# A retention pair's matmuls put in another order: three changes of tile mode instead of five

## Chip, core and metric

The kernel runs on one core of one Trainium2 chip. The metric is the device time of one execution in microseconds (us). Below, PE is TensorE, DVE is VectorE, ACT is ScalarE, POOL is GpSimd and SP is SyncE, whose queue issues nearly all DMAs of the stage in question.

## Reference

Retention (attention with a decay instead of a softmax) over 4 batches of 8 heads of 64 features and 576 positions; then a gated layer and a layer of eight experts, which the change leaves alone.

```python
scores = scale * np.matmul(q, k.transpose(0, 1, 3, 2))
gamma = 1.0 - 2.0 ** (-5.0 - np.arange(H))
rel = pos[:, None] - pos[None, :]
Dmat = np.where(rel >= 0, gamma[:, None, None] ** rel[None, :, :], 0.0)
ret = np.matmul(scores * Dmat[None], v)
...
x = ret.transpose(0, 2, 1, 3).reshape(B * S, H * D)
x = _moe_ref(x=x, ...)          # RMS norm, silu(x wg) * (x wv), wo
return _moe2_ref(x=x, ...)      # 8 experts, Sinkhorn-normalised weights
```

## The kernel before

The program has three stages: retention (about the first 85 of 2000 us), the gated layer, the experts. Only retention is touched. It goes over 16 pairs of heads (4 batches times 4 pairs); the two heads of a pair lie in partitions 0 to 63 and 64 to 127. The 576 positions are four chunks of 128 and a tail of 64. For pair i the work is:

- `scores(i)`: eight matmuls of a chunk's keys with its queries (contraction 64, output 128 rows, so PE works as tiles of 64 x 128) into `sc`, two PSUM banks; two matmuls for the tail's scores (64 x 64 tiles) into slot 4 of `u`; DVE multiplies `sc` by the masks into `am` (L293).
- `states(i)`: eight matmuls of keys with values (contraction 128, output 64 rows: tiles of 128 x 64) into slots 0 to 3 of `u`; DVE scans them over the chunks into `block_states` (L313) and masks the tail's scores into `mt` (L314).
- `outputs(i)`: the tail's output (from the state and from `mt`, 64 x 64 tiles) into slot 5 of `u`; the states' share of the chunks (64 x 64 tiles) and the masked scores' share (128 x 64 tiles) into `o`, one bank; DVE scales both into `acc` (L342 for the tail, L344 for the chunks).

So one tile `u`, a single PSUM bank of 512 fp32 columns, holds a pair's chunk states, its tail scores and its tail output. `u`, `sc` and `o` have two buffers each, `kT` and `ks` two, `qT` and `vs` three.

The loop of L453 runs one pair ahead: in turn i it records `scores(i + 1)`, `states(i + 1)` and `outputs(i)`, then one step of the gated layer's weight preparation on DVE and ACT (L126 to L146), then a step of the RMS norm where its sums are ready. The order in which this is written is the order on each engine; semaphores follow from which tile is read and written. Two instructions of different engines on one PSUM bank are kept apart by the recording layer, whichever columns they touch. The loads of a turn stand on SP's queue in this order: `qT` and `vs` of pair i + 2, a weight tile where a slot is free, `kT` and `ks` of pair i + 3. Each waits for the last reader of the buffer that it fills, and those behind it wait with it.

Of the kernel before, what the change touches and what calls it, by code (L numbers as in the profile page):

```python
# [13 lines left out]
ALU = mybir.AluOpType  # L14
# [3 lines left out]
B, H, S, D = 4, 8, 576, 64  # L18
# [7 lines left out]
C = 128  # L26
NC = S // C
# [23 lines left out]
def retention_glu_experts(ctx: ExitStack, tc: tile.TileContext, a, out):  # L51
# [6 lines left out]
    nc = tc.nc  # L58
# [43 lines left out]
    def load_weights(most=2):  # L102
        for _ in range(most):
            if n_load[0] == len(sources) or not raw_slots:
                return
            i = n_load[0]
            n = raw_of[i] = raw_slots.pop(0)
            t = rawp.tile([128, 1024], I32, tag=f"raw{n}", name=f"raw{i}")
            nc.sync.dma_start(t, sources[i].bitcast(I32))
            raw[i], asked[i] = t, n_step[0]  # L110
            n_load[0] += 1
# [139 lines left out]
    steps = acc_d[:, :, (B - 1) * S:(B - 1) * S + D * NC]  # L251
# [3 lines left out]
    heads = [slice(h * D, (h + 1) * D) for h in range(2)]  # L255
    loaded, staged, squares = {}, {}, {}

    def load_pair(i, *names, queue=nc.sync):
        if i >= B * NP:
            return  # L260
        b, pr = divmod(i, NP)
        t = {}
        for n in names:
            t[n] = ld.tile([128, a[n].shape[-1]], F32, tag=n, name=f"{n}{i}", bufs=2 if n[0] == "k" else 3)
            queue.dma_start(t[n], a[n][b, pr])
        loaded.setdefault(i, {}).update(t)

    def scale_keys(i):
        if i >= B * NP:
            return  # L270
        for h in range(2):
            hh = 2 * (i % NP) + h
            ks = loaded[i]["ks"].rearrange("p (c h d) -> p c h d", h=2, d=D)[:, :, h, :]
            nc.scalar.mul(ks, ks, g_key[:, hh:hh + 1])

    def scores(i):
        if i >= B * NP:
            return
        pr = i % NP
        t = loaded[i]  # L280
        kt, qt = t["kT"], t["qT"]
        u = psa.tile([128, 512 // D, D], F32, tag="u", name=f"u{i}")
        sc = psa.tile([128, 2, NC, C], F32, tag="sc", name=f"sc{i}")
        am = am_p.tile([128, 2, NC, C], F32, tag="am", name=f"am{i}")
        for c in range(NC):
            for h in range(2):
                hs = slice(h * D, (h + 1) * D)
                cs = slice(c * C, (c + 1) * C)
                nc.tensor.matmul(sc[:, h, c, :], lhsT=kt[hs, cs], rhs=qt[hs, cs], start=True, stop=True)
        for h in range(2):  # L290
            hs = slice(h * D, (h + 1) * D)
            nc.tensor.matmul(u[hs, NC, :], lhsT=kt[hs, NC * C:], rhs=qt[hs, NC * C:], start=True, stop=True)
        nc.vector.tensor_mul(am, sc, masks[:, pr].to_broadcast([128, 2, NC, C]))  # L293
        staged[i] = am, u

    def by_chunk(u):
        return u[:, :NC, :].rearrange("p c d -> p (c d)")

    def states(i):
        if i >= B * NP:  # L300
            return
        pr = i % NP
        t = loaded[i]
        am, u = staged[i]
        ks, vs = t["ks"], t["vs"]
        by_feature = by_chunk(u).rearrange("p (d c) -> p d c", c=NC)
        for c in range(NC):
            for h in range(2):
                cs = slice((2 * c + h) * D, (2 * c + h + 1) * D)
                nc.tensor.matmul(by_feature[h * D:(h + 1) * D, :, c], lhsT=ks[:, cs], rhs=vs[:, cs], start=True, stop=True)  # L310
        st = block_states[i % 2]
        mt = am_p.tile([128, TAIL], F32, tag="mt", name=f"mt{i}")
        nc.vector.tensor_tensor_scan(st, steps[:, pr], by_chunk(u), 0.0, ALU.mult, ALU.add)  # L313
        nc.vector.scalar_tensor_tensor(mt, u[:, NC, :], g_tail[:, pr:pr + 1], causal_t, ALU.mult, ALU.mult)  # L314
        staged[i] = am, mt, st, u

    def outputs(i):
        b, pr = divmod(i, NP)
        t = loaded.pop(i)
        qt, vs = t["qT"], t["vs"]  # L320
        am, mt, st, u = staged.pop(i)
        st = st.rearrange("p (d c) -> p d c", c=NC)
        o = psa.tile([128, NC, C], F32, tag="o", name=f"o{i}")
        ot = u[:, NC + 1, :]
        for hs in heads:
            nc.tensor.matmul(ot[hs, :], lhsT=st[hs, :, NC - 1], rhs=qt[hs, NC * C:], start=True, stop=False)
        for hs in heads:
            nc.tensor.matmul(ot[hs, :], lhsT=vs[hs, 2 * NC * D:], rhs=mt[hs, :], start=False, stop=True)
        for c in range(1, NC):
            for hs in heads:  # L330
                nc.tensor.matmul(
                    o[hs, c, :], lhsT=st[hs, :, c - 1], rhs=qt[hs, c * C:c * C + C],
                    start=c == 1, stop=False, skip_group_check=True,
                )
        for c in range(NC):
            for h, hs in enumerate(heads):
                nc.tensor.matmul(
                    o[hs, c, :], lhsT=vs[:, (2 * c + h) * D:(2 * c + h + 1) * D], rhs=am[:, h, c, :],
                    start=False, stop=c == NC - 1, skip_group_check=True,
                )  # L340
        xf = acc_d[:, pr, b * S:(b + 1) * S]
        nc.vector.tensor_mul(xf[:, NC * C:], ot, g_out[:, pr, :TAIL])  # L342
        yield
        nc.vector.tensor_mul(  # L344
            xf[:, :NC * C].rearrange("p (c i) -> p c i", c=NC), o,
            g_out[:, pr:pr + 1, :].to_broadcast([128, NC, C]),
        )
        sq = sp.tile([128, S], F32, tag="sq", name=f"sq{i}")
        nc.scalar.activation(sq, xf, AF.Square)
        if pr:  # L350
            nc.gpsimd.tensor_add(sq, sq, squares[b])
        squares[b] = sq
        yield
# [93 lines left out]
    scale_keys(0)  # L447
    scale_keys(1)
    scores(0)
    states(0)  # L450
    load_pair(2, "kT", "ks")
    for i in range(B * NP):
        b, pr = divmod(i, NP)  # L453
        load_pair(i + 2, "qT", "vs")
        load_weights(1)
        if i == 2:
            nc.sync.dma_start(rms_g, a["rms_g"])
            nc.sync.dma_start(ident, a["ident"])
            nc.sync.dma_start(wg_raw.rearrange("p k e -> p (k e)"), a["wg"])
        scores(i + 1)  # L460
        states(i + 1)
        load_pair(i + 3, "kT", "ks")
        scale_keys(i + 2)
        out_steps = outputs(i)
        next(out_steps)
        step_weights(load=False, apart=1)
        next(out_steps)
        if i in SUMS_AT:
            next(sums[i // NP - 1], None)
        if i >= 2 * NP - 1:  # L470
            next(norms[0], None)
        if i in (B * NP - 3, B * NP - 1):
            next(norms[1])
# [729 lines left out]
    n, l = len(jobs) - 1, len(jobs) - 2  # L1203
# [108 lines left out]
```

## Time and profile before

| what | us |
|---|---|
| median of 3 runs (lowest, highest) | 2000.55 (2000.46, 2002.4) |
| span of the profiled execution (first to last instruction) | 1999.9 |
| the profiled execution's own time, where a run's time is the span and what lies around it | not listed; 2000.55 less 1999.9 leaves 0.65 |
| PE busy | 1983.4 (99%) |
| DVE busy | 1441.8 (72%) |
| ACT busy | 869.7 (43%) |
| retention's last matmul gives way to the norm's | 84.35 after the start |

PE's busy time includes stretches in which it is slowed by its neighbours, since matmuls are pipelined and their ends are modelled. Times in the rows are counted from the start of the span.

### The profile page before, as it was taken

To read this page: it belongs to the slowest core of one execution; us is meant where nothing else is said; L and a number is where in the kernel's file an instruction comes from. 1 tells how busy PE (TensorE), PEld (TensorE's weight loads), DVE (VectorE), ACT (ScalarE), POOL (GpSimd) and SP (SyncE) were. 2 spreads that over 40 slices of the span, in tenths; PEclk is the share of its full clock that TensorE was granted. 3 is DMA by queue.
4 is the path that set the end of the run, shared out by engine and by line. 5 is a ranking of instruction groups with operands and counts; after the bars stand their busy time and mean duration, and the time that the engine had idled before them with its cause. 6 is when DMAs were issued, how large, how long until landed. Compare 5 with 4: busy or idle time off the path is not lost.

```text
span 1999.9 us, 29898 instructions
## 1 busy us (share of the span) xinstructions
PE 1983.4 (99%) x11390; PEld 1856.2 (93%) x11390; DVE 1441.8 (72%) x2276; ACT 869.7 (43%) x1655; POOL 740.4 (37%) x692
## 2 busy tenths in 40 slices
PE   9999999999999999999999999999999999999998
PEld 7788988988889998999999999999999999999998
DVE  6865555554688777777786777777787777777777
ACT  4453323322454444444444444444445444444443
POOL 3300000000153544545544444545466454444543
PEclk9999999999999999999999999999999999999999
DMA  9411111110178888888888676767767767676773
GB/s 314 150 32 53 50 45 52 44 43 1 48 294 301 291 301 305 308 295 311 303 309 313 245 279 239 276 254 263 265 237 282 264 256 280 237 266 251 271 260 142
DMA packets 111535, 436.56 MB, mean 218 GB/s; under 512 B 11720, under 2 KB 29128, under 8 KB 95008
## 3 DMA queue, kind: packets, MB, share of 16 engines
q1 hardware_dynamic: 109904, 432.39, 59.5%
q8 instruction: 89, 1.46, 0.3%
q10 hardware_dynamic: 1248, 1.49, 0.2%
q0 software_dynamic: 240, 0.79, 0.1%
q14 instruction: 54, 0.44, 0.1%
HBM read 312.41 MB, written 122.21 MB: 217 GB/s over the span
## 4 chain that ended last, share of the span: by engine, by line
PE 95%; DVE 3%; DMA 1%; ACT 1%; POOL 0%; issue 0%; ACTq 0%; SPq 0%; DVEq 0%; POOLq 0%
PE py L751 10%; PE pz L751 10%; PE px L751 10%; PE qx L997 7%; PE qy L997 6%; PE qz L997 6%; PE gv L177 5%; PE gv L179 5%; PE gv L178 5%; PE y L178 4%; PE y L179 4%; PE y L177 4%; PE qz L751 3%; PE x L177 2%; PE x L178 2%; PE x L179 2%
## 5 line engine op out<-in xcount | busy, mean ns | idle before, releaser
L751 PE MATMUL py<-sx,w1s 128*128 128x384 f32 x1152 | 232.0, 335 | 1.1 <-ACT py L1089 0.9
L539 POOL TENSOR_TENSOR t<-rw 128x256 f32<-128x256 f32 x32 | 43.0, 1343 | 508.2 <-DVE sx L576 398.8
L1178 POOL TENSOR_TENSOR acc<-z,a_block 128x384 f32<-128x384 f32 x63 | 64.0, 1015 | 434.7 <-DVE z L1172 434.7
L751 PEld LDWEIGHTS py<-sx,w1s 128*128 128x128 f32 x1152 | 203.0, 188 | 5.3 <-ACT py L1089 2.4
L751 PE MATMUL px<-xhi,w1s 128*128 128x384 f32 x640 | 188.8, 335 | 0.3 <-DVE t L205 0.3
L987 ACT CAST xhi<-acc 128x384 fp32r<-128x384 f32 x316 | 156.0, 514 | 69.8 <-POOL acc L1178 35.4
L991 DVE TENSOR_TENSOR xlo<-acc,xhi 128x384 fp32r<-128x384 f32 x191 | 178.3, 960 | 1.8 <-ACT xhi L987 1.8
L991 POOL TENSOR_TENSOR xlo<-acc,xhi 128x384 fp32r<-128x384 f32 x125 | 145.7, 1165 | 29.7 <-ACT xhi L987 29.7
L1005 DVE TENSOR_TENSOR acc<-acc,qz 128x384 f32<-128x384 f32 x246 | 134.9, 548 | 25.5 <-PE qz L997 25.4
L205 DVE TENSOR_TENSOR t<-t,gv 128x512 f32<-128x512 f32 (+1 forms) x60 | 38.0, 633 | 124.6 <-PE gv L179 123.3
L751 PEld LDWEIGHTS px<-xhi,w1s 128*128 128x128 f32 x640 | 117.9, 188 | 0.9 <-DVE t L205 0.6
L1005 DVE TENSOR_TENSOR acc<-acc,qx 128x384 f32<-128x384 f32 x123 | 67.4, 548 | 71.1 <-PE qx L997 71.1
L751 PE MATMUL pz<-sx,w1s 128*128 128x384 f32 x576 | 115.4, 334 | 0.0
L751 PE MATMUL pz<-xhi,w1s 128*128 128x384 f32 x384 | 113.9, 337 | 0.1
L796 DVE SCALAR_TENSOR_TENSOR acc<-y,prob,acc 128x512 f32<-128x512 f32 x144 | 101.4, 742 | 8.1 <-PE y L179 8.1
L751 PE MATMUL px<-xlo,w1s 128*128 128x384 f32 x320 | 107.0, 334 | 0.0
L1023 ACT COPY qz<-qy 128x384 f32<-128x384 f32 x127 | 58.8, 463 | 106.3 <-PE qy L997 100.5
L179 PE MATMUL y<-xlo,xhi 128*128 128x512 f32 x264 | 103.8, 393 | 0.0
L178 PE MATMUL y<-xlo,xhi 128*128 128x512 f32 x264 | 103.6, 393 | 0.0
L177 PE MATMUL y<-xlo,xhi 128*128 128x512 f32 x264 | 102.6, 389 | 0.0
L751 PEld LDWEIGHTS pz<-sx,w1s 128*128 128x128 f32 x576 | 101.3, 188 | 0.7
L1015 ACT COPY qy<-qx 128x384 f32<-128x384 f32 x127 | 58.8, 463 | 95.2 <-PE qx L997 89.4
(401 smaller groups left out, 5890.9 us busy)
## 6 DMA issues: line engine op xcount, KB each, us to landing
w1s<-w_kept SPq DMA_DIRECT2D x64, 1792.0 KB, 7.2
w_kept<-w1s SPq DMA_DIRECT2D x32, 1792.0 KB, 6.6
rw<-in_w_dram SPq DMA_DIRECT2D x64, 512.0 KB, 5.5
w_kept<-xlo SPq DMA_DIRECT2D x64, 512.0 KB, 3.8
w2s<-w_kept SPq DMA_DIRECT2D x32, 1024.0 KB, 6.8
w_extra<-w_kept SPq DMA_DIRECT2D x32, 768.0 KB, 7.7
w_kept<-xlo SPq DMA_DIRECT2D x44, 384.0 KB, 4.3
w2c<-w_kept SPq DMA_DIRECT2D x32, 512.0 KB, 7.9
```

What stands on the lines that cost most here:

```text
L177: nc.tensor.matmul(ps, lhsT=lh, rhs=rh, start=start, stop=False)
L178: nc.tensor.matmul(ps, lhsT=lh, rhs=rl, start=False, stop=False)
L179: nc.tensor.matmul(ps, lhsT=ll, rhs=rh, start=False, stop=stop)
L751: nc.tensor.matmul(ps, lhsT=l, rhs=r[:, k, :], start=start and k == 0 and i == 0, stop=k == 1 and i == 2, skip_group_check=True,)
L796: nc.vector.scalar_tensor_tensor(o, y_2, pe, o, ALU.mult, ALU.add)
L987: nc.scalar.copy(hi, x)
L991: (engine or nc.vector).tensor_sub(lo, x, f32(hi))
L997: nc.tensor.matmul(ps, lhsT=l, rhs=r, start=start and i == 0, stop=i == 2, skip_group_check=True)
L1005: nc.vector.tensor_add(dst, dst, ps)
L1015: nc.scalar.copy(y, x)
L1023: nc.scalar.copy(z, y)
L1178: nc.gpsimd.tensor_add(sums[0], z[:, 0, :], h_blocks[0])
```

## The change

In a turn the matmuls of both pairs are put in another order. The tail's scores move from `scores` to a second step of `states`, behind the chunk states and their scan. The masked scores' share of the output moves to the front of `outputs`, and is recorded between the two steps of `states`. `states` and `outputs` become generators that the loop steps in turn; the loads of `kT` and `ks` and the scaling of `ks` are recorded between these steps. The accumulation in `o` now starts with the masked share and ends with the states' share. No instruction is added or removed.

```diff
@@ scores
-        for h in range(2):
-            hs = slice(h * D, (h + 1) * D)
-            nc.tensor.matmul(u[hs, NC, :], lhsT=kt[hs, NC * C:], rhs=qt[hs, NC * C:], start=True, stop=True)
         nc.vector.tensor_mul(am, sc, masks[:, pr].to_broadcast([128, 2, NC, C]))
@@ states
         st = block_states[i % 2]
+        nc.vector.tensor_tensor_scan(st, steps[:, pr], by_chunk(u), 0.0, ALU.mult, ALU.add)
+        yield
+        for hs in heads:
+            nc.tensor.matmul(u[hs, NC, :], lhsT=kt[hs, NC * C:], rhs=qt[hs, NC * C:], start=True, stop=True)
         mt = am_p.tile([128, TAIL], F32, tag="mt", name=f"mt{i}")
-        nc.vector.tensor_tensor_scan(st, steps[:, pr], by_chunk(u), 0.0, ALU.mult, ALU.add)
         nc.vector.scalar_tensor_tensor(mt, u[:, NC, :], g_tail[:, pr:pr + 1], causal_t, ALU.mult, ALU.mult)
         staged[i] = am, mt, st, u
+        yield
@@ outputs
+        for c in range(NC):
+            for h, hs in enumerate(heads):
+                nc.tensor.matmul(
+                    o[hs, c, :], lhsT=vs[:, (2 * c + h) * D:(2 * c + h + 1) * D], rhs=am[:, h, c, :],
+                    start=c == 0, stop=False, skip_group_check=True,
+                )
+        yield
         for hs in heads:
             nc.tensor.matmul(ot[hs, :], lhsT=st[hs, :, NC - 1], rhs=qt[hs, NC * C:], start=True, stop=False)
...
                 nc.tensor.matmul(
                     o[hs, c, :], lhsT=st[hs, :, c - 1], rhs=qt[hs, c * C:c * C + C],
-                    start=c == 1, stop=False, skip_group_check=True,
-                )
-        for c in range(NC):
-            for h, hs in enumerate(heads):
-                nc.tensor.matmul(
-                    o[hs, c, :], lhsT=vs[:, (2 * c + h) * D:(2 * c + h + 1) * D], rhs=am[:, h, c, :],
                     start=False, stop=c == NC - 1, skip_group_check=True,
                 )
@@ the loop
         scores(i + 1)
-        states(i + 1)
+        state_steps, out_steps = states(i + 1), outputs(i)
+        next(state_steps, None)
+        next(out_steps)
         load_pair(i + 3, "kT", "ks")
         scale_keys(i + 2)
-        out_steps = outputs(i)
+        next(state_steps, None)
         next(out_steps)
```

Three places show what stands on the engines. The first is PE in turn 2, where pair 3 is scored and pair 2 put out, before the change. A number behind a name is the pair; the words in brackets are the engines or DMA queues whose signal an instruction waits for.

```order
L289 MATMUL sc3_326<-qT3_255,kT3_226 128x128 [waits DMAHW7_49,DMAHW1_49]
L289 MATMUL sc3_326<-qT3_255,kT3_226 128x128 x7
L292 MATMUL u3_325<-qT3_255,kT3_226 64x64 [waits DVE_49]
L292 MATMUL u3_325<-qT3_255,kT3_226 64x64
L310 MATMUL u3_325<-vs3_257,ks3_228 64x64 [waits DMAHW2_49,DMAHW0_49,Activation_49]
L310 MATMUL u3_325<-vs3_257,ks3_228 64x64 [waits Activation_49]
L310 MATMUL u3_325<-vs3_257,ks3_228 64x64 x6
L326 MATMUL u2_261<-qT2_195,block_states0_115 64x64 x2
L328 MATMUL u2_261<-mt2_283,vs2_197 64x64 x2
L331 MATMUL o2_356<-qT2_195,block_states0_115 64x128 x6
L337 MATMUL o2_356<-am2_263,vs2_197 64x128 x8
```

The same turn of PE with the change:

```order
L289 MATMUL sc3_326<-qT3_255,kT3_231 128x128 [waits DMAHW7_49,DMAHW1_49]
L289 MATMUL sc3_326<-qT3_255,kT3_231 128x128 x7
L307 MATMUL u3_325<-vs3_257,ks3_233 64x64 [waits DMAHW0_49,DMAHW2_49,DVE_49,Activation_49]
L307 MATMUL u3_325<-vs3_257,ks3_233 64x64 [waits Activation_49]
L307 MATMUL u3_325<-vs3_257,ks3_233 64x64 x6
L328 MATMUL o2_346<-am2_263,vs2_197 64x128 x8
L312 MATMUL u3_325<-qT3_255,kT3_231 64x64 [waits DVE_49]
L312 MATMUL u3_325<-qT3_255,kT3_231 64x64
L334 MATMUL u2_261<-qT2_195,block_states0_115 64x64 x2
L336 MATMUL u2_261<-mt2_299,vs2_197 64x64 x2
L339 MATMUL o2_346<-qT2_195,block_states0_115 64x128 x6
```

The tail's scores (L292, now L312) moved behind the masked share (L337, now L328), and the first of them waits for a signal of DVE that it did not wait for there. In the built program that signal is the scan's of the same pair: for pair 0 it is DVE's third, after a memset and the mask product, for pair 1 its sixth. The wait that stood on L292, for the buffer of `u`, stands on the chunk states now.

The second place is the end of the stage on PE, pairs 14 and 15, from the scores of pair 15's tail on. Before:

```order
L292 MATMUL u15_1150<-qT15_1071,kT15_1034 64x64 [waits DVE_49]
L292 MATMUL u15_1150<-qT15_1071,kT15_1034 64x64
L310 MATMUL u15_1150<-vs15_1073,ks15_1036 64x64 [waits DMAHW2_49,DMAHW0_49,Activation_49]
...
L326 MATMUL u14_1075<-qT14_1005,block_states0_115 64x64 x2
L328 MATMUL u14_1075<-mt14_1097,vs14_1007 64x64 x2
L331 MATMUL o14_1175<-qT14_1005,block_states0_115 64x128 x6
L337 MATMUL o14_1175<-am14_1077,vs14_1007 64x128 x8
L326 MATMUL u15_1150<-qT15_1071,block_states1_116 64x64 [waits DVE_49]
```

With the change:

```order
L328 MATMUL o14_1171<-am14_1077,vs14_1007 64x128 x8
L312 MATMUL u15_1150<-qT15_1071,kT15_1039 64x64 [waits DVE_49]
L312 MATMUL u15_1150<-qT15_1071,kT15_1039 64x64
L334 MATMUL u14_1075<-qT14_1005,block_states0_115 64x64 x2
L336 MATMUL u14_1075<-mt14_1109,vs14_1007 64x64 x2
L339 MATMUL o14_1171<-qT14_1005,block_states0_115 64x128 x6
L328 MATMUL o15_1207<-am15_1152,vs15_1073 64x128 [waits PE_49]
```

Pair 14's share from the states stood ahead of anything that waits for pair 15's scan, and stands behind it now.

The third place is SP's queue at the loads of pairs 2 and 3. Before:

```order
L265 DMA kT_191<-in_kT_dram 128x576 [waits DMAHW2_49,PE_49]
L265 DMA ks_193<-in_ks_dram 128x512 [waits DMAHW3_49,PE_49,Activation_49]
L265 DMA qT_195<-in_qT_dram 128x576 [waits DMAHW4_49]
L265 DMA vs_197<-in_vs_dram 128x576 [waits DMAHW5_49]
L109 DMA raw_199<-in_gate_dram 128x1024 [waits DMAHW6_49]
L265 DMA kT_226<-in_kT_dram 128x576 [waits DMAHW7_49,PE_49]
```

With the change:

```order
L265 DMA kT_191<-in_kT_dram 128x576 [waits DMAHW2_49,PE_49]
L265 DMA ks_193<-in_ks_dram 128x512 [waits DMAHW3_49,Activation_49]
L265 DMA qT_195<-in_qT_dram 128x576 [waits DMAHW4_49]
L265 DMA vs_197<-in_vs_dram 128x576 [waits DMAHW5_49]
L109 DMA raw_199<-in_gate_dram 128x1024 [waits DMAHW6_49]
L265 DMA kT_231<-in_kT_dram 128x576 [waits DMAHW7_49,PE_49]
```

The order of the queue is the same. The load of `kT` waits, then as now, for the tail's scores of the pair whose buffer it takes; these come later on PE, so a wait of its own of `ks` on PE is no longer needed.

## Rows read from the trace of the kernel before

**Rows 1.** The page, busy time by engine (us, share, instructions).

```profile
PE 1983.4 (99%) x11390; PEld 1856.2 (93%) x11390; DVE 1441.8 (72%) x2276; ACT 869.7 (43%) x1655; POOL 740.4 (37%) x692
```

**Rows 2.** Busy time in two stretches (length; each engine's us and instructions; PEclk, DMA share, GB/s).

```profile
27.04:31.30 4.26, 4.26 (x75) 3.71 (x73) 3.81 (x7) 2.40 (x5) 1.42 (x1) 1.00 0.89 277
...
57.82:81.16 23.34, 21.47 (x354) 18.61 (x354) 23.09 (x43) 12.18 (x25) 7.83 (x6) 1.00 0.59 195
```

**Rows 3.** Timeline, pair 4 scored, pair 3 put out (start, us, instruction, idle before).

```profile
22.79 1.16 PE L289 MATMUL sc<-qT,kT 64*128 64x128 f32 x16
...
23.88 0.33 PE L292 MATMUL u<-qT,kT 64*64 64x64 f32 x4
24.00 1.23 DVE L293 TENSOR_TENSOR am<-sc,masks 128x1024 f32<-128x1024 f32 x1
...
24.14 0.69 PE L310 MATMUL u<-vs,ks 128*64 128x64 f32 x16
...
24.76 0.45 PE L326 MATMUL u<-qT,block_states 64*64 64x64 f32 x4
...
25.05 0.28 PE L328 MATMUL u<-mt,vs 64*64 64x64 f32 x4
...
25.14 0.68 DVE L313 TENSOR_TENSOR_SCAN block_states<-acc,u 128x256 f32<-128x256 f32 x1
25.16 0.93 PE L331 MATMUL o<-qT,block_states 64*64 64x128 f32 x12
25.73 0.26 DVE L314 SCALAR_TENSOR_TENSOR mt<-u,tables 128x64 f32<-128x64 f32 x1
...
26.02 1.09 PE L337 MATMUL o<-am,vs 128*64 128x128 f32 x16
26.04 0.42 DVE L126 TENSOR_SCALAR cv<-cv 128x512 f32<-128x512 f32 x1
...
27.04 0.97 PEld L289 LDWEIGHTS sc<-qT,kT 64*128 64x128 f32 x16 [0.17 <-issue]
...
27.44 0.68 DVE L344 TENSOR_TENSOR acc<-o,g_out 128x512 f32<-128x512 f32 x1
```

**Rows 4.** Timeline, a load of queries on SP's queue; then all such loads' times to landing.

```profile
26.13 0.33 SPq L265 DMA_DIRECT2D qT<-in_qT_dram  x1
...
DMA to landing us min/median/max: 3.3/4.7/6.6
```

**Rows 5.** Timeline of the first two pairs.

```profile
7.08 0.33 PE L292 MATMUL u<-qT,kT 64*64 64x64 f32 x4
...
8.48 0.69 DVE L313 TENSOR_TENSOR_SCAN block_states<-acc,u 128x256 f32<-128x256 f32 x1
...
8.82 0.42 SPq L265 DMA_DIRECT2D qT<-in_qT_dram  x1
...
14.28 1.16 PE L289 MATMUL sc<-qT,kT 64*128 64x128 f32 x16 [1.64 <-DMA qT<-in_qT_dram]
```

**Rows 6.** Timeline from 61 to 87 us, DVE and PE.

```profile
62.86 1.97 DVE L412 TENSOR_TENSOR xlo<-acc,xhi 128x576 fp32r<-128x576 f32 x1
...
65.89 0.67 DVE L313 TENSOR_TENSOR_SCAN block_states<-acc,u 128x256 f32<-128x256 f32 x1
...
66.66 0.21 DVE L342 TENSOR_TENSOR acc<-u,g_out 128x64 f32<-128x64 f32 x1
66.79 0.68 DVE L146 TENSOR_TENSOR wslots<-cv,wslots 128x512 fp32r<-128x512 f32 x1
...
66.92 0.33 PE L292 MATMUL u<-qT,kT 64*64 64x64 f32 x4 [0.64 <-DVE acc L342]
...
74.30 0.75 DVE L412 TENSOR_TENSOR xlo<-acc,xhi 128x576 fp32r<-128x576 f32 x1
...
80.03 1.21 DVE L293 TENSOR_TENSOR am<-sc,masks 128x1024 f32<-128x1024 f32 x1
...
84.35 1.13 PE L399 MATMUL rb<-dg,ones 128*128 128x512 f32 x2
```

More of the change, by code (lines that the diff above doesn't have):

```diff
@@ L304, in states @@
         am, u = staged[i]
-        ks, vs = t["ks"], t["vs"]
+        kt, qt, ks, vs = (t[n] for n in ("kT", "qT", "ks", "vs"))
         by_feature = by_chunk(u).rearrange("p (d c) -> p d c", c=NC)
@@ L449, in retention_glu_experts @@
     scores(0)
-    states(0)
+    for _ in states(0):
+        pass
     load_pair(2, "kT", "ks")
```

## Prediction

> **What bounds the kernel now.** I read the page first, then busy time by stretches, then the timeline of one turn, then the waits at both ends of retention. PE is busy in 99% of the span [rows 1], so what retention gains or loses on PE reaches the end; nothing behind it makes up for a delay. Retention itself has two regimes. From the scores of pair 2 (14.28 [rows 5]) to those of pair 11, shortly before 57.82 and nine turns later, PE sets the pace: in the turn from 27.04 PE is busy for all of 4.26 us, DVE for 3.81, and the DMA engines stand at 0.89 [rows 2]. From pair 11's mask product to pair 15's scan (57.82 to 81.16, four turns) DVE is busy for 23.09 of 23.34 us and sets it [rows 2]. So three resources lie close together, and a change that helps one of them can give little.
>
> One PE-bound turn, counted from the start S of its scores [rows 3]: scores to 1.09, tail scores to 1.35, chunk states to 1.97, tail output from the state to 2.26 and from `mt` to 2.37, states' share to 3.23, masked share to 4.25. DVE runs beside it: the mask product from 1.21, the scan from 2.35 to 3.03 (25.14 and 0.68, less 22.79), `mt` from 2.94. Neither engine waits for the other within a turn, as the scan of the pair being scored is used by PE only in the next turn.
>
> **The change, part by part.** *Two tile-mode changes fewer.* The states' 16 instructions of 64 columns take 0.62, where four like them (L328, start to start of what follows) take 0.11, so 0.44 for 16: 0.18 is left over. The tail scores take 0.26 for four: 0.15 left. The weight load of the scores sits idle for 0.17 behind the masked share [rows 3]. I take 0.15 to 0.18 for a change of mode, 0.33 for the two that go. The Trainium skill (TensorEngine Tiling (Array Packing), Tiling Modes) says that changing the tiling mode drains the engine; the rows agree, and if that alone counted, 15 turns at 0.33 would give some 5 us back.
>
> *A wait that was not there.* The tail's scores now stand behind the scan of their own pair and write the same PSUM bank that the scan reads; in the built program the first of them waits for that scan. PE arrives there at 1.09 + 0.44 + 1.02 = 2.55 after S. The scan cannot end earlier than 1.21 + 1.14 (mask product, start to start) + 0.68 = 3.03, and PE takes up a DVE result 0.05 later (66.66 + 0.21 to 66.92) [rows 3, 6]. So PE waits 0.53 in each turn, with pair i's tail output, its states' share and the next scores queued behind, and the first mode change saved only lengthens that wait: it is worth nothing, and would be worth its 0.18 if the scan were done by 2.55. The Trainium skill (PSUM — Partial Sum Buffer, PSUM bank collisions raise a hardware error) asks for a semaphore by bank and quadrant, not by address, which is why columns that nobody else touches still wait; no row of before has such a wait, since there the tail's scores came ahead of the scan.
>
> *The PE-bound turn.* A loop now closes within a turn. Call M the start of the tail scores. Behind them stand 0.11 (four of L328's kind, no mode change), 0.29, 0.11 and 0.86 (the rows' distances from L326 to L337), so the next scores start at M + 1.37; the mask product 1.21 later; the scan's end 1.14 + 0.68 later; 0.05 to PE. Together 4.45 against 4.25 now (22.79 to 27.04) [rows 3]: +0.20, in nine turns **+1.8 us**.
>
> *DVE behind the scan.* `mt` and the tail's scaling (L342) follow the scan on DVE and now wait for PE's tail scores and tail output. L342 starts at M + 0.40 + 0.28 + 0.05 = M + 0.73, and the weight step at M + 0.86 (0.13 later, 66.66 to 66.79) [rows 3, 6]. Queued behind these two are that weight step, L344 and the next mask product. Where the weight step has three instructions (1.40, from 26.04 to 27.44) L344 ends at 0.86 + 1.40 + 0.59 = M + 2.85 instead of the M + 2.58 at which the next mask product could start [rows 3]. That is +0.27 in three turns (the fourth such turn has a norm product on PE that leaves DVE the time): **+0.8 us**.
>
> *The DVE-bound turns.* Now 0.90 lies from the scan's start to the weight step's (65.89 to 66.79). Then it is 0.67 + 0.05 + 0.86 = 1.58. DVE has no other idle time there, so the 0.68 adds to each of four turns: **+2.7 us** [rows 6]. Against it: L412 took 1.97 at one place and 0.75 at another [rows 6]; I guess that the long one shares time with POOL's work, and if the shift parts them up to 1.2 comes back. I take none of it.
>
> *The end.* From pair 15's mask product (80.03) to the norm's matmul (84.35) are 4.32 us [rows 6]. Pair 14's states' share was done by then; now it stands behind pair 15's scan. The new path is 1.14 + 0.68 + 0.05 to M, 1.37 to the masked share of pair 15, 1.02 for it, and 0.29 + 0.11 + 0.86 for the rest [rows 3]: 5.52, so **+1.2 us**.
>
> *The start, and the loads.* The load of `kT` for pair 2 waits for pair 0's tail scores, which ran at 7.08 and now wait for the scan that ended at 8.48 + 0.69 = 9.17 [rows 5]. Behind it on SP stand `ks`, `qT` and `vs` of pair 2, a weight tile, and pair 3's `kT`. `qT` of pair 2 was issued at 8.82, and pair 2's scores waited 1.64 for it until 14.28 [rows 5]. The bounds: the whole 2.1 from 7.08 to 9.22 is added to 14.28; or the load lands no later, because the DMA engines are shared with fewer loads, and PE's own loop (9.22, 0.26 for the tail scores, 4.45 for pair 1) would bring pair 2 in at 13.93, 0.3 sooner. I take +0.7, nearer to the lower end, as the load's 5.3 from issue to use holds well over 1 us of queueing (3.3 is the least such load takes [rows 4]): **+0.7 us**.
>
> In the steady turns the load of `qT` is issued when the states' share has read its buffer. That was at 26.13 for scores at 31.30, 5.17 later [rows 2, 4]. Now the states' share ends the turn, so what is left is one turn, 4.45. In turns without a weight tile that is enough by the least landing (3.3), not by the median (4.7) [rows 4]; but the median holds the crowded first turns. I take nothing for it and keep it as a rival.
>
> **The sum.** 1.8 + 0.8 + 2.7 + 1.2 + 0.7 = +7.2 us. Made against the profiled execution, 1999.9 + 7.2 = 2007.1 of span; that span lies 0.65 under the median of the runs, so 2000.55 + 7.2 = **2007.8 us**, +0.36%. Its own range comes from the bounds of the terms: start -0.3 to +2.1, the weight steps 0 to +0.8, the four DVE-bound turns 2.7 less 1.2 to 2.7; that is +4.2 to +8.6, 2004.8 to 2009.2.
>
> **The rivals.**
> *Queries come late.* If `qT` lands as the median does, 4.7 after issue, PE waits 0.25 in each of the nine turns; in the turns behind a weight tile, where landing went up to 6.6, some 2 us more in each of one to three of them [rows 4]. For it: `kT`, `ks`, `qT` and `vs` are now issued within some 1.5 us of each other, where they were spread over a turn. Against it: a longer turn leaves the DMA engines more time per pair. Price +2.2 to +6; with the sum some 2012.
> *Idle time of DVE takes up part of it.* If most of the weight steps, the start and the shared L412 come out at their low ends and the round trip from scan to tail is shorter than the rows make it, the sum falls to +2 to +4: about 2003.5. Against it: the loop of 4.45 is made of rows that hardly vary from turn to turn.
> *The modes win.* If the wait for the scan did not hold PE, a PE-bound turn would lose 0.33. The place is the first tail-score matmul, and it decides there: a scan that ended by S + 2.55 would free it. The DVE-bound turns gain nothing, so nine turns give -3.0, about 1997.6. This is what the page on tiling would have one expect. Against it: a mask product cannot start before the scores end, and that already puts the scan's end at S + 3.03 [rows 3].
>
> **How the numbers follow.** The forecast has 0.60, late queries 0.20, the partly hidden loss 0.13, the win of the modes 0.07. A measurement of this kernel can tell about 0.2% (4 us) from no change. Forecast and late queries are both slower by more than that: 0.80; the partly hidden loss counts as the same: 0.13; faster: 0.07. The range has to reach into the late queries and into the partly hidden loss until 0.2 is left out: 2003 to 2012.5.
>
> **What would show it.** In the profile after: PE idle of about 0.5 us before L312 in each PE-bound turn, put down to DVE's scan (L309); DVE idle of 0.3 to 0.5 before `mt` (L314) and again before L344's tail scaling; scores 4.4 to 4.5 apart at the undisturbed turns; the norm's matmul near 91.5 instead of 84.35; all later stages unchanged in length. The prediction is wrong if PE shows no wait at L312, if turns are shorter than 4.25, or if the waits for `qT` add up to several us.

## The result, and the profile after

The changed kernel takes 2013.64 us (median of 4 runs, 2012.52 to 2021.56) against 2000.86 of the kernel before in the same session (4 runs). The ratio is 1.0071, 95% interval 1.0058 to 1.0083: slower by 0.7%, as forecast in sign and kind, but by 12.8 us where I forecast 7.2. The profiled execution has a span of 2012.5, 12.6 more than before.

The page's row of busy time hardly shows this: PE is busy 0.6 us longer than in [rows 1], at the same 99%.

```profile
PE 1984.0 (99%) x11390; PEld 1857.6 (92%) x11390; DVE 1447.0 (72%) x2276; ACT 869.4 (43%) x1655; POOL 738.9 (37%) x692
```

In the profiled execution all of the loss lies ahead of the gated layer. Its first matmul starts at 85.80 before and 98.40 after, and what follows takes 1914.1 us in both (1999.9 less 85.80, 2012.5 less 98.40).

The timeline of one undisturbed turn, PE and DVE (start, us, instruction, idle before), answers to [rows 3]:

```profile
40.74 1.16 PE L289 MATMUL sc<-qT,kT 64*128 64x128 f32 x16
...
41.83 0.69 PE L307 MATMUL u<-vs,ks 128*64 128x64 f32 x16
41.95 1.23 DVE L290 TENSOR_TENSOR am<-sc,masks 128x1024 f32<-128x1024 f32 x1 [0.67 <-PE sc L289]
42.35 1.05 PE L328 MATMUL o<-am,vs 128*64 128x128 f32 x16
43.09 0.68 DVE L309 TENSOR_TENSOR_SCAN block_states<-acc,u 128x256 f32<-128x256 f32 x1
43.82 0.33 PE L312 MATMUL u<-qT,kT 64*64 64x64 f32 x4 [0.43 <-DVE block_states L309]
43.99 0.40 PE L334 MATMUL u<-qT,block_states 64*64 64x64 f32 x4
44.20 0.28 DVE L314 SCALAR_TENSOR_TENSOR mt<-u,tables 128x64 f32<-128x64 f32 x1 [0.44 <-PE u L312]
...
44.55 0.23 DVE L344 TENSOR_TENSOR acc<-u,g_out 128x64 f32<-128x64 f32 x1
44.69 0.68 DVE L146 TENSOR_TENSOR wslots<-cv,wslots 128x512 fp32r<-128x512 f32 x1
45.20 0.71 PE L289 MATMUL sc<-qT,kT 64*128 64x128 f32 x8
```

Read it from PE's only bracket: the tail's scores (L312) idle for 0.43 and are released by the scan (L309), which ends at 43.77, 3.03 after the scores began. The turn is 4.46 long. Everything behind L312 keeps the distances of the forecast: L344 at 0.73 and the weight step at 0.87 after it, the next scores at 1.38.

What was not forecast is further on. Windows (length; busy time by engine; PEclk, DMA share, GB/s) from one scoring to the next, pairs 11 to 15, the last to the norm's matmul:

```profile
61.32:65.78 4.46, 4.03 (x75) 3.55 (x73) 3.69 (x8) 2.27 (x5) 2.56 (x2) 1.00 0.90 301
65.78:74.02 8.24, 4.66 (x75) 3.96 (x73) 7.22 (x13) 3.44 (x6) 1.60 (x1) 0.90 0.68 221
74.02:79.34 5.32, 4.88 (x74) 4.36 (x72) 4.16 (x8) 2.73 (x5) 2.78 (x2) 0.83 0.60 195
79.34:87.03 7.69, 5.59 (x85) 5.08 (x83) 7.12 (x14) 2.67 (x5) 0.00 (x0) 0.94 0.46 150
87.03:95.76 8.73, 8.73 (x110) 7.76 (x109) 5.58 (x16) 3.87 (x9) 2.90 (x3) 0.66 0.12 31
```

PEclk was 1.00 in [rows 2]; here it is below 1.00 in the last four windows, 0.66 in the last. The PE rows around the first fall show what went ahead of it:

```profile
67.39 1.05 PE L328 MATMUL o<-am,vs 128*64 128x128 f32 x16
72.02 0.33 PE L312 MATMUL u<-qT,kT 64*64 64x64 f32 x4 [3.58 <-DVE block_states L309]
...
72.58 1.50 PE L339 MATMUL o<-qT,block_states 64*64 64x128 f32 x12
74.02 2.02 PE L289 MATMUL sc<-qT,kT 64*128 64x128 f32 x16
```

PE stood idle for 3.58 us, since DVE, at work all the while, had not come to that pair's scan. Then the states' share takes 1.50 instead of 0.93 and the scores 2.02 instead of 1.16. After a wait of 2.10 at 84.09 it is the same (scores at 87.03: 2.08).

At the end of the stage, the timeline of POOL, PE and DVE (the norm's matmul, L401, answers to L399 in [rows 6]):

```profile
95.40 1.79 POOL L353 TENSOR_TENSOR sq<-sq,sq 128x576 f32<-128x576 f32 x1 [4.90 <-ACT sq L351]
95.76 1.12 PE L401 MATMUL rb<-dg,ones 128*128 128x512 f32 x2
95.86 1.89 DVE L132 SCALAR_TENSOR_TENSOR cv<-raw,cv 128x512 int32<-128x512 int32 x1
97.67 0.68 DVE L346 TENSOR_TENSOR acc<-o,g_out 128x512 f32<-128x512 f32 x1
98.40 0.50 PE L177 MATMUL gv<-xhi,wslots 128*128 128x512 f32 x1 [1.16 <-DVE acc L346]
```

The gated layer's first matmul waits 1.16 for the last scaling of the chunks, which stands behind a weight instruction of 1.89 on DVE. Before, 1.45 lay between the norm's matmul and this one; now 2.64. The same instruction stood there before too, but took 0.69: it began at 84.45, ahead of POOL's sum at 84.57, and now begins behind that sum. The 1.20 more are the whole of the difference.

### The profile page after: what moved, and what is told of

It reads as the page before. It is cut to its first block, busy times and chain, and to the rows that moved or that the text cites. A ratio compares the mean times of both kernels' runs of the same rounds, so it can differ in the third digit from the quotient of the medians.

```text
span 2012.5 us, 29900 instructions
## 1 busy us (share of the span) xinstructions
PE 1984.0 (99%) x11390; PEld 1857.6 (92%) x11390; DVE 1447.0 (72%) x2276; ACT 869.4 (43%) x1655; POOL 738.9 (37%) x692
## 3 DMA queue, kind: packets, MB, share of 16 engines
q8 instruction: 89, 1.46, 0.3%
## 4 chain that ended last, share of the span: by engine, by line
PE 94%; DVE 4%; DMA 1%; ACT 1%; issue 0%; POOL 0%; SPq 0%; ACTq 0%; DVEq 0%
PE pz L756 10%; PE py L756 10%; PE px L756 10%; PE qx L1002 6%; PE qy L1002 6%; PE qz L1002 6%; PE gv L177 5%; PE gv L178 5%; PE gv L179 5%; PE y L178 4%; PE y L179 4%; PE y L177 4%; PE qz L756 3%; PE x L177 2%; PE x L178 2%; PE x L179 2%
```

## The experiments

Three explanations were to be told apart. **First**, the wait for the scan closes a loop through PE and DVE (the forecast). **Second**, loads come late. **Third**, the long waits of PE lower its clock, and slow matmuls then stand on the path. Positions in one table (us from the start of the span; "turn" is scores to scores where nothing but the program's own order holds PE):

| kernel | turn | scores of pair 2 | of pair 11 | norm's matmul | gated layer | ratio to before [95%] |
|---|---|---|---|---|---|---|
| before | 4.25 | 14.28 | 56.61 | 84.35 | 85.80 | |
| after | 4.46 | 14.85 | 61.32 | 95.76 | 98.40 | 1.0071 [1.0058, 1.0083] |
| e0_again | 4.46 | 14.19 | 63.35 | 96.84 | 99.48 | 1.0070 [1.0053, 1.0087] |
| e1_scan_last | 3.96 | 13.95 | 59.44 | 87.32 | 89.24 | 1.0007 [0.9998, 1.0017] |
| e2_filled | 4.46 | 15.89 | 61.88 | 93.28 | 95.92 | 1.0050 [1.0035, 1.0065] |
| e3_tail_apart | 4.46 | 14.41 | 60.76 | 95.18 | 97.82 | 1.0056 [1.0041, 1.0071] |
| e4_bank | 3.96 | 14.74 | 60.51 | 90.92 | 93.56 | 1.0034 [1.0021, 1.0047] |
| e5_four | 4.11 | 15.48 | 57.65 | 85.38 | 86.83 | 1.0003 [0.9994, 1.0012] |
| e6_wait_alone | 5.48 | 15.24 | 68.33 | 109.09 | 110.89 | 1.0128 [1.0113, 1.0143] |
| e7_scan_last_tail_apart | 3.96 | 12.86 | 56.18 | 84.25 | 85.97 | 1.0004 [0.9994, 1.0013] |
| e8_small_first | 3.96 | 14.21 | 57.29 | 85.88 | 87.33 | 1.0007 [0.9998, 1.0016] |
| e9_small_first_steps | 3.96 | 14.18 | 56.16 | 85.23 | 87.16 | 1.0005 [0.9996, 1.0014] |
| e10_both | 4.46 | 13.53 | 59.95 | 91.34 | 93.97 | 1.0044 [1.0027, 1.0060] |
| e11_last_step | 4.46 | 15.87 | 61.93 | 97.10 | 98.52 | 1.0060 [1.0045, 1.0075] |

**The changed kernel once more (e0_again).** No edit.

> The changed kernel as it is, once more, as the yardstick for the three that run beside it. All theories: 12 to 13 us over the kernel before, PE waiting for the scan at the tail scores in 15 turns, one turn near 20 us with a wait for queries of some 1.8 us, and PE's granted clock near 0.5 to 0.6 of full around 73 to 76 and 86 to 92 us.

Measured 2016.05. The undisturbed turn repeats to 0.01 us, but the excess moves: PE waits for the scan in 11 turns, not in 15; pair 6, not pair 4, waits for its queries (1.93); the granted clock is 0.66 from 63 to 68 and 0.50 from 75 to 80. Toward the end it stays at 1.00, though PE waits 2.11 for the scan at 87.44 as it did at 84.09 in the profile above. What lies beyond the loop is not the same in every execution.

**The scan behind the tail's scores (e1_scan_last).** Against the changed kernel:

```diff
-        nc.vector.tensor_tensor_scan(st, steps[:, pr], by_chunk(u), ...)
         yield
         for hs in heads:
             nc.tensor.matmul(u[hs, NC, :], lhsT=kt[hs, NC * C:], ...)
+        nc.vector.tensor_tensor_scan(st, steps[:, pr], by_chunk(u), ...)
```

> The changed kernel's order on PE, with one edit: the scan of the chunk states is recorded behind the tail scores, so DVE's scan waits for PE's tail scores and PE's tail scores no longer wait for the scan. Theory 1 (the loss is the wait for the scan and what it drags along: the loop within a turn, the round trip on DVE, the low clock): no wait before the tail scores, PE-bound turns of 3.9 to 4.3 us, clock 1.00 through retention, total 1997 to 2001. Theory 2 (the loss is in the loads that are issued later): their places are as in the changed kernel, so the waits for queries stay or grow, total 2004 to 2010.

Measured 2003.44, not told apart from before and between the ranges of the two theories, so the turn has to decide. PE and DVE:

```profile
39.86 1.16 PE L289 MATMUL sc<-qT,kT 64*128 64x128 f32 x16
...
42.45 0.33 PE L311 MATMUL u<-qT,kT 64*64 64x64 f32 x4
...
42.83 0.69 DVE L312 TENSOR_TENSOR_SCAN block_states<-acc,u 128x256 f32<-128x256 f32 x1 [0.53 <-PE u L311]
...
43.82 0.94 PE L289 MATMUL sc<-qT,kT 64*128 64x128 f32 x12
```

The order of PE is the changed one, and the turn is 3.96: without the wait, two mode changes give back 0.29. So the wait for the scan costs 0.50 a turn (4.46 less 3.96), and nearly all of the loss goes with it. But no gain remains: PE now waits 6.4 us in all for queries, and pair 11 is scored later than before. Nor did the clock stay at 1.00, as theory 1 had it: it was 0.54 from 79.7 to 83.

**Queries or keys too late? The tail of the keys apart (e3_tail_apart, e7_scan_last_tail_apart).** The keys of the tail get a tile and a load of their own, with three buffers, so the large load of keys and those behind it on SP's queue wait no longer for the tail's scores. e3 does this to the changed kernel, e7 to e1:

```diff
+            w = NC * C if n == "kT" else a[n].shape[-1]
-            t[n] = ld.tile([128, a[n].shape[-1]], ...); queue.dma_start(t[n], a[n][b, pr])
+            t[n] = ld.tile([128, w], ...); queue.dma_start(t[n], a[n][b, pr][:, :w])
+            if n == "kT":
+                t["kt"] = ld.tile([128, TAIL], F32, tag="kt", bufs=3, ...)
+                queue.dma_start(t["kt"], a[n][b, pr][:, w:])
```

> The changed kernel with the keys' tail of 64 columns loaded into a tile of its own with three buffers, so that the load of the 512 other columns waits for the chunk scores as before and no longer for the tail scores; one small load more per pair. Theory 2 (late loads): the queue goes on early, the wait for queries of 1.8 us in the turn near 20 us and the later start of pair 2 go, total 2 to 3 us below the changed kernel. Theory 1 (the scan): the waits for the scan stay in all turns and the total stays 9 us or more above the kernel before.

Measured 2013.70, which is 2.35 below e0_again in the same session and level with the first measurement of the changed kernel. The waits of e3 to 110 us (us in total, times, longest) leave the scan's as they were; the queries' were 3.9 in 3 in the profile of the changed kernel:

```profile
PE u L316 <- DVE block_states L313: 12.6, 15, 3.6
...
PE sc L293 <- DMA qT<-in_qT_dram: 2.1, 3, 1.1
```

That the edit took them away is not shown. The same loop without it has 3.3 in e0_again, 1.8 in e11 and 1.0 in e2, and with it 2.3 in e10: these waits differ more between executions than with the edit.

> Scan recorded behind the tail's scores, and the last 64 columns of the keys in a tile of their own with three buffers, so that the big load of keys waits no longer for the tail's scores. With the scan behind the tail's scores alone, PE waited 6.4 us for queries and pair 11 was scored at 59.44. If the late load of keys, which holds up SP's queue, made those waits, they fall to 3 or less and pair 11 is scored at 56 to 57; DVE's turns behind it then take part of it back, and the time is 1997 to 2001. If the waits come from queries issued late in their own right (the states' share ends the turn) or from DMA engines that are full, they stay at 5 or more and the time stays at 2001 to 2004.

Measured 2002.29. The waits for queries fell from 6.4 to 3.1, and pair 11 is scored at 56.18 instead of 59.44. That fits a late load of keys that holds up the queue, with one profile of each. Yet the kernel is no faster than before. Busy time from pair 2's scores to pair 11's, before and in e7:

```profile
14.28:56.61 42.33, 42.01 (x672) 36.22 (x673) 34.00 (x69) 21.60 (x44) 9.62 (x7) 1.00 0.92 305
```

```profile
12.86:56.18 43.32, 39.69 (x674) 34.88 (x673) 35.22 (x71) 21.56 (x46) 9.62 (x7) 1.00 0.92 303
```

PE has 2.3 us less to do and the stretch is no shorter, with the DMA engines at 0.92 in both (305 and 303 GB/s). That the DMA engines are now the bound fits these rows; it was not tried with fewer bytes.

**PE kept busy in the long waits (e2_filled).** Behind the masked share of turns 11, 12 and 13 the changed kernel runs 14, 5 and 9 matmuls of a constant, whose output nobody reads:

```diff
+    def fill(i):
+        for _ in range({11: 14, 12: 5, 13: 9}.get(i, 0)):
+            nc.tensor.matmul(o_of_sc, lhsT=idle, rhs=idle_512, start=True, stop=True)
...
         next(out_steps)
+        fill(i)
         load_pair(i + 3, "kT", "ks")
```

> The changed kernel with extra matmuls that compute nothing used (14, 5 and 9 of 128x128 bf16 weights by 512 columns into a bank already read) ahead of the tail scores in turns 11, 12 and 13, where PE sat idle for 3.58 and 2.10 us. Theory 3 (the idle time there lowered PE's clock and the slow matmuls after it cost time of their own): clock 1.00 through retention, the mask products of pairs 13 and 15 each some 1.2 us sooner, the end some 1 us sooner, total 3 to 4.5 us below the changed kernel. Rival (DVE sets the pace there and the slow matmuls lie beside it): total within 1 us of the changed kernel.

Measured 2013.02. Each of the four runs (2009.82 to 2014.87) is below those of e0_again in the same session (2015.08 to 2017.82), by 3.0 in the medians as theory 3 had it; but the first session's runs of the changed kernel begin at 2012.52, and other waits differ. The window from pair 11's scores to the norm's matmul decides, first of the changed kernel, then of e2:

```profile
61.32:95.76 34.44, 27.89 (x409) 24.70 (x407) 27.78 (x55) 14.98 (x30) 9.84 (x8) 0.85 0.50 164
```

```profile
61.88:93.28 31.40, 29.96 (x437) 23.42 (x435) 27.50 (x55) 14.96 (x30) 9.78 (x8) 1.00 0.56 180
```

28 matmuls more and 3.04 us less (2.09 less than e0_again): the fallen clock cost 2 to 3 us. What is left, 31.40 against 27.74 before, is +3.66.

**Both suspects taken out (e10_both).** The changed kernel with the edits of e2 and e3.

> The changed order with both suspects besides the scan wait taken out: filler matmuls keep PE busy in the waits of turns 11 to 13 (extra work whose output nobody reads), and the last 64 columns of the keys have a tile of their own. If the terms of the prediction are the rest of it, the granted clock is 1.00 from 60 us to the norm's matmul, waits for queries are under 1.2 in sum, pair 11 is scored at 59.5 to 60.5, the norm's matmul stands at 91 to 92.5, and the time is 7 to 9 us over before, the 1.2 at the hand-over to the gated layer among it. If the clock and the queries add little, it stays 11 or more over before.

Measured 2009.8, 8.0 over before. The granted clock is 1.00 in every window, the norm's matmul stands at 91.34:

```profile
59.95:91.34 31.39, 29.92 (x437) 23.39 (x435) 27.50 (x55) 14.91 (x30) 9.78 (x8) 1.00 0.52 170
```

The forecast had 91.5 there. The later part (31.39) agrees by its own terms. The earlier part agrees in sum only: pair 2 came 0.75 earlier than before, where e3 with the same load of keys has 0.13 later, and the nine turns hold 2.3 of waits for queries, where under 1.2 were expected.

**The tail's scores in another bank (e4_bank).** They go into the bank of `sc`, behind the mask product, and `mt` reads them there; the scan stays ahead of them.

```diff
-            nc.tensor.matmul(u[hs, NC, :], lhsT=kt[hs, NC * C:], ...)
+            nc.tensor.matmul(sc[hs, 0, 0, :TAIL], lhsT=kt[hs, NC * C:], ...)
-        nc.vector.scalar_tensor_tensor(mt, u[:, NC, :], ...)
+        nc.vector.scalar_tensor_tensor(mt, sc[:, 0, 0, :TAIL], ...)
```

> The changed kernel with one edit: the tail scores are written into the bank of the same pair's chunk scores, once the mask product has read them, instead of the bank that is being scanned. They then wait for the mask product, which ends 0.7 us sooner, and no longer for the scan. Theory 1 (the shared bank closes the loop): PE's wait ahead of the tail scores is near 0 in the PE-bound turns, undisturbed turns of 3.9 to 4.0 us, DVE's wait between scan and tail mask near 0; total 4 to 8 us below the changed kernel, with waits for queries taking up part of the gain as in the run with the scan behind the tail scores. Rival (the order itself, not the bank, makes the loop): within 2 us of the changed kernel.

Measured 2009.08. In an undisturbed turn the tail's scores run while the scan does:

```profile
43.48 0.68 DVE L309 TENSOR_TENSOR_SCAN block_states<-acc,u 128x256 f32<-128x256 f32 x1
43.71 0.33 PE L312 MATMUL sc<-qT,kT 64*64 64x64 f32 x4
```

So it is the shared bank that holds PE, not the data, and the turn is 3.96 again. More than half of the loss in time stays all the same. Of the 7.8 by which the gated layer starts later than before, 3.9 lie ahead of pair 11, where PE now waits over 5 us for loads (2.26 of it at 26.60). Another 2.7 lie in the DVE-bound turns: there L312 waits for the mask product, 3.0 at the longest, and the granted clock is 0.50 from 70 to 74. The rest is the hand-over.

**The wait without the new order (e6_wait_alone).** The kernel before, with the tail's scores behind the chunk states and the scan; the masked share stays last.

```diff
@@ scores
-            nc.tensor.matmul(u[hs, NC, :], lhsT=kt[hs, NC * C:], ...)
@@ states
         nc.vector.tensor_tensor_scan(st, steps[:, pr], by_chunk(u), ...)
+        for hs in heads:
+            nc.tensor.matmul(u[hs, NC, :], lhsT=kt[hs, NC * C:], ...)
```

> The order of before, with one thing moved: the tail's scores stand behind the chunk states and the scan of their own pair, and the masked share stays last. So the wait comes without the new order. If the wait is the cause, PE comes to the tail scores at S + 1.53 and waits to S + 3.08; behind that stand 0.11, 0.29, 0.11, 0.86 and 1.02 and the mode changes, so undisturbed turns are 5.4 to 5.6 long, 1.2 more than before, nine of them +11, and with the other stages as in the changed kernel the time is some 2014 to 2020. If the wait costs little and the order of the matmuls or the loads are the cause, turns stay under 4.5 and the time under 2009. If idle time lowers the clock wherever PE waits for long, the granted clock falls in some of the waits of 1.5 us too, and the time goes past 2020.

Measured 2027.27, above the 2014 to 2020 of the first theory. Turns are 5.48 as worked out, 1.30 of it the wait:

```profile
29.40 0.33 PE L312 MATMUL u<-qT,kT 64*64 64x64 f32 x4 [1.30 <-DVE block_states L310]
```

Pair 11 is scored 11.7 later, as the first theory had it. The rest of the loss, 13.0 more from there to the norm's matmul, is more than its terms: PE waits up to 3.9 there, and the clock falls for longer. In the turns with a wait of 1.30 it does not fall, against the third possibility in the expectation:

```profile
26.32:68.33 42.01, 32.87 (x530) 28.19 (x528) 29.48 (x57) 18.09 (x37) 8.20 (x6) 1.00 0.71 227
...
98.39:109.09 10.70, 9.83 (x109) 8.46 (x109) 6.29 (x15) 3.99 (x9) 3.55 (x3) 0.56 0.17 49
```

**One mode change fewer, no new wait (e5_four).** The kernel before, with the tail's scores between the chunk states and the scan: four changes of mode.

```diff
@@ scores
-            nc.tensor.matmul(u[hs, NC, :], lhsT=kt[hs, NC * C:], ...)
@@ states
+        for hs in heads:
+            nc.tensor.matmul(u[hs, NC, :], lhsT=kt[hs, NC * C:], ...)
         nc.vector.tensor_tensor_scan(st, steps[:, pr], by_chunk(u), ...)
```

> The kernel before with one edit: the tail scores stand behind the chunk states and ahead of the tail output, still ahead of the scan. One tile-mode change fewer per turn, no new wait of PE; the load of keys starts some 0.5 us later in the turn. If a mode change costs what the rows of before make it (0.15 to 0.18): undisturbed PE-bound turns of 4.07 to 4.12 instead of 4.25, total 0 to 1.5 us below the kernel before. If the later load decides: waits for queries grow and the total is 0 to 2 us above it.

Measured 2002.48, the same as before. The turn is 4.11 (42.86 to 46.97), 0.14 less than 4.25. The start of pair 2 is 1.2 later, behind a wait of 1.94 for queries.

**All 64 by 64 groups behind the scores (e8_small_first, e9_small_first_steps).** The order is scores, tail's scores, tail output, states' share, then chunk states and masked share: three changes of mode, and the scan has time until the next turn. e9 also records the tail's scaling and the weight step ahead of the chunk states.

```diff
@@ outputs, behind the states' share
+        yield
@@ the loop
         scores(i + 1)
+        out_steps = outputs(i)
+        next(out_steps)
         states(i + 1)
```

> The kernel before with another order that also has three mode changes: chunk scores, then all 64 by 64 groups (tail scores, tail output, states' share), then chunk states and masked share. Tail scores stand ahead of the scan, and queries are let go of in mid-turn. Theory 1: no wait for the scan, undisturbed PE-bound turns of 3.9 to 4.0, clock 1.00. Theory 2 (loads): queries are issued sooner than in any other order here, so their waits stay below 1 us each and the total comes out 1 to 3 us below the kernel before, unless DVE, whose scan starts 0.6 us later in the turn, holds the turns with three weight instructions at 4.6; then it is within 1 us of the kernel before.

> The run before this one with DVE's order changed: tail scaling and weight step are recorded between mask product and scan, where DVE would wait for the chunk states. Theories 1 and 2 alike: turns with three weight instructions of 4.0 to 4.3, total 2 to 4 us below the kernel before. If waits for loads take the place: no better than the kernel before.

Measured 2003.05 and 2002.90, neither told apart from before by 0.2%. Turns are 3.96 in both. In e8 from pair 2 to pair 11 it still takes 43.08 against 42.33 before, with waits of 2.5 in all for queries and 1.6 for one DVE result. The granted clock was not 1.00 throughout: 0.62 from 68.5 to 73, behind a wait of 2.18. From pair 11 to the norm's matmul, where DVE sets the pace, it takes 28.59 and 29.07 against 27.74. A turn that is 0.29 shorter on PE brings nothing that can be measured here.

**One weight step moved in the last turn (e11_last_step).**

```diff
+        if i < B * NP - 1:
             step_weights(load=False, apart=1)
         next(out_steps)
+        if i == B * NP - 1:
+            step_weights(load=False, apart=1)
```

> The changed kernel, with one step of the weight preparation in the last turn of retention recorded behind the last scaling of the chunks instead of ahead of it. If the gated layer's first matmul waits for that scaling only because a weight instruction of 1.89 us stands ahead of it on DVE, the wait of 1.16 goes and the first matmul stands 1.4 to 1.5 us behind the start of the norm's matmul instead of 2.64; in the time that is 1.2 us less, at the edge of what can be measured. If the wait has another cause (the PSUM buffers of the gated layer, or the norm), it stays at 2.6.

Measured 2014.17. The timeline at the end of the stage:

```profile
97.10 1.13 PE L401 MATMUL rb<-dg,ones 128*128 128x512 f32 x2
97.22 0.69 DVE L346 TENSOR_TENSOR acc<-o,g_out 128x512 f32<-128x512 f32 x1 [0.54 <-PE o L339]
97.83 0.94 DVE L146 TENSOR_TENSOR wslots<-cv,wslots 128x512 fp32r<-128x512 f32 x1
...
98.52 0.50 PE L177 MATMUL gv<-xhi,wslots 128*128 128x512 f32 x1
```

1.42 from the norm's matmul to the gated layer instead of 2.64, and no wait: the long weight instruction ahead of the scaling was the cause. In the time it does not show: the norm's matmul came 1.34 later in this execution than in the changed kernel's profile, of it 1.02 by pair 2's scores.

## Why the prediction came out as it did

The sum of the terms was +7.2; the profiled execution has +12.6. Of the 5.4 that the sum lacks, 2.8 come with the fallen clock, 1.5 from waits for queries and 1.2 from the hand-over to the gated layer.

| term | forecast | measured |
|---|---|---|
| start, to pair 2's scores | +0.7 | +0.57 |
| nine turns to pair 11's scores (1.8 and 0.8) | +2.6 | +4.14, of it 1.78 a wait for queries |
| pair 11's to pair 15's mask product | +2.7 | +4.41 |
| pair 15's mask product to the norm's matmul | +1.2 | +2.29 |
| norm's matmul to the gated layer | none | +1.19 |

Pair 15's mask product, first in the changed kernel and then in e2:

```profile
89.15 1.23 DVE L290 TENSOR_TENSOR am<-sc,masks 128x1024 f32<-128x1024 f32 x1 [1.09 <-PE sc L289]
```

```profile
87.76 1.21 DVE L290 TENSOR_TENSOR am<-sc,masks 128x1024 f32<-128x1024 f32 x1
```

- *The wait for the scan* was right in place and size, also against its rival, the win of the modes. The turn of 4.45 and, with a weight step of three instructions, of 4.72 came as 4.45 to 4.46 and 4.73 (30.36 to 35.09). e1 and e4 take the wait away in two ways, and the turn falls to 3.96. PE's idle time is 0.43 instead of 0.53, as the masked share's matmuls reach 0.10 further; that changes nothing in a turn that ends with the scan.
- *The mode changes* were read as 0.15 to 0.18 each and cost 0.14 (e5) to 0.15 (e1). e1, e5, e7, e8 and e9 show what the forecast left out: even with no wait for the scan they win nothing in the total, as waits for loads and then DVE take the place.
- *"I take nothing for it"*, of the queries in the steady turns, was the first step that failed. In one turn the load was issued 4.66 before PE came to it (25.91 less the wait of 1.78, less 19.47), near the 4.45 forecast, but was used only 6.44 after its issue:

```profile
19.47 0.33 SPq L265 DMA_DIRECT2D qT<-in_qT_dram  x1
...
25.91 1.16 PE L289 MATMUL sc<-qT,kT 64*128 64x128 f32 x16 [1.78 <-DMA qT<-in_qT_dram]
```

  Less the 0.32 that the kernel before waits in these turns, this is 1.46, and without such waits the nine turns come to +2.68 against 2.6. So the rival of the late queries, whose price began at 2.2, took place in part, on top of the forecast and not instead of it. That its time of 2012 is near the measured one is luck: all waits for queries grew by 1.0 (3.9 against 2.9). Why this load took 6.44 stays open: the waits move from one execution to the next, and the late load of keys is one cause for which e7 speaks and e3 does not.
- *"DVE has no other idle time there, so the 0.68 adds"* and *the end* were the second, and the larger. The terms are right while the clock is at 1.00. In e2 the first is +2.46 against 2.7, and the end takes 5.52 (87.76 to 93.28), the path as it was worked out; e0_again has 5.52 there too, with the clock at 1.00. In the changed kernel the two come to +6.70 instead of 3.9. The forecast saw that DVE would wait for PE, but not the reverse: with the tail's scores behind the scan PE can no longer run ahead in DVE's turns, stands idle for 3.58 and 2.10, and comes back at a lower clock just where DVE waits for it. The sum has no term for a clock below 1.00. The guess that L412 might give 1.2 back fell too: that instruction (now L414) took 1.96 again.
- *The end* also had no term for the hand-over: +1.19, the weight instruction that now runs beside POOL's sum; e11 shows it.
- *The start* came out near its +0.7 partly by luck. The same loop brings pair 2 in 0.09 earlier than before in e0_again, and 1.61 and 1.59 later in e2 and e11.
- *Slips that change little:* the load of pair 2's queries was used 5.46 after its issue (8.82 to 14.28), not 5.3; the 0.59 from L344's start to its end stands in none of the rows; and 2.2 with some 2 more in each of up to three turns makes up to 8, not 6.
- *What would show it:* waits at L312 and L314, distances and turns came as written. Before L344's tail scaling there was idle time in two turns only (0.17 and 0.36). The norm's matmul did not come as written: 95.76 instead of 91.5. The stages behind it are unchanged.

No version here is measurably faster than the kernel before.

## What to carry to other kernels

Before a matmul group is moved for the sake of tile modes, look at which PSUM bank it writes and who else reads that bank then: an engine-to-engine round trip inside a turn (0.50 here) outweighs two mode changes (0.29). Where another engine sets the pace, PE's freedom to run ahead is worth keeping even though PE is not the bound: a PE that had to wait for long can come back slow and then be the bound. And where several engines are near full (here PE 99%, the DMA engines 92% and DVE 80% from pair 2 to pair 11), a gain on one of them is to be priced at nothing until the others have been shown to have room.

## What the hardware showed that was not expected

**The clock behind idle time.** After PE had been idle for 3.58 us, the granted clock was 0.57 in the 4 us that followed, so mostly the lower of its two levels, 1.2 of 2.4 GHz:

```profile
68.40:72.00 3.60, 0.03 (x2) 0.00 (x0) 3.56 (x3) 2.12 (x4) 1.22 (x1) 1.00 0.76 297
72.00:76.00 4.00, 3.98 (x42) 3.48 (x42) 2.52 (x5) 1.09 (x2) 0.33 (x1) 0.57 0.57 163
```

It also fell behind 2.10 us here and 2.21 in e6. That idle time is a cause is shown by e2 and e10: with matmuls in these waits the clock is 1.00 from pair 11's scores to the norm's matmul. But its length alone does not decide. The clock stayed at 1.00 through e6's waits of 1.30 in every turn, through one of 2.16 in e7, and behind 2.11 in e0_again:

```profile
87.50:90.00 2.50, 2.50 (x35) 2.35 (x35) 2.09 (x6) 0.86 (x2) 0.00 (x0) 1.00 0.03 10
```

And it fell to 0.54 in e1 behind a wait of 0.99, and to 0.57 in e2 at 40.2, where no wait of the turn ahead was longer than 0.43; in both, ten matmuls of one column each (L378 in e1, L379 in e2) had just run, as they do elsewhere without a fall (88.81 in e0_again). What else decides is not settled by these runs. The Trainium skill (TensorE: Matmul & The Clock Gate, HAM oscillation — how this bites in real kernels) describes a matmul kernel whose clock falls back at each of its waits for a DMA; behind the wait of 3.58 us the trace agrees, with DVE in place of the DMA.

**DVE beside POOL.** The weight instruction L132, 0.68 alone, took 1.89 while POOL added two tiles (95.40 to 97.19), and ended at 97.75, 0.56 after POOL. L414 with 1.96 ended at 70.24, 0.63 after such a sum of POOL's:

```profile
68.01 1.60 POOL L353 TENSOR_TENSOR sq<-sq,sq 128x576 f32<-128x576 f32 x1 [3.20 <-ACT sq L351]
68.28 1.96 DVE L414 TENSOR_TENSOR xlo<-acc,xhi 128x576 fp32r<-128x576 f32 x1
```

Before, where DVE's L132 began first, it was POOL's sum that took longer, 1.85 instead of 1.41 at 80.01:

```profile
84.45 0.69 DVE L132 SCALAR_TENSOR_TENSOR cv<-raw,cv 128x512 int32<-128x512 int32 x1
84.57 1.85 POOL L351 TENSOR_TENSOR sq<-sq,sq 128x576 f32<-128x576 f32 x1 [2.02 <-ACT sq L349]
```

So whichever of the two comes second seems to do most of its work only when the first is done. The mask product, which reads one input from PSUM, is not lengthened beside POOL (1.23 at 41.95). The Trainium skill (Trainium Architecture — The Big Picture, What this means for kernel authors) says that DVE and GpSimd share a port pair under an exclusive lock; these rows agree, though no run here parted the two for that purpose.
